# A third tile in the ring for finished blocks, output weights in five single steps, and row maxima as three and one: an attention and feed-forward block on one core

## The chip, the core and the metric

The kernel runs on one core of a Trainium2 chip. Such a core has five engines that run side by side, each with its own queue of instructions, taken in order: TensorE (PE in the profile, its weight loads PEld), VectorE (DVE), ScalarE (ACT), GpSimd (POOL) and SyncE (SP), which here only starts transfers. PE writes its results to PSUM; DVE and ACT read them there and put them into SBUF. Transfers between SBUF and the memory of the chip (DMA) are started from an engine's queue, here those of SP and ACT. Engines wait for each other and for transfers through semaphores. The metric is the time of one execution on the device in microseconds (us); the kernel before takes 2186.95 us as the median of 3 runs (2176.08 to 2189.83).

## The reference

The reference is a transformer block with layer norm ahead of each part, for 2048 tokens of width 640, 32 heads of 20 numbers each, and a feed-forward width of 1728. Cut to its core:

```python
# x: [1, 2048, 640]; wqkv: [640, 1920]; wo: [640, 640]
# w_gate, w_up: [640, 1728]; w_down: [1728, 640]
def attention(x):
    qkv = (x @ wqkv).reshape(B, S, 3, H, Dh).transpose(2, 0, 3, 1, 4)
    q, k, v = qkv[0], qkv[1], qkv[2]
    scores = einsum("bhqd,bhkd->bhqk", q, k) * Dh ** -0.5
    p = softmax(scores, axis=-1)
    o = einsum("bhqk,bhkd->bhqd", p, v)
    return o.transpose(0, 2, 1, 3).reshape(B, S, D) @ wo

h = x + attention(layernorm(x))
out = h + (silu(layernorm(h) @ w_gate) * (layernorm(h) @ w_up)) @ w_down
```

The softmax subtracts the maximum of each row of scores. The kernel finds these maxima in a pass of its own, with scores that are computed for that alone.

## The kernel before

Operands of the matmuls are split in two parts, a rounded one ("hi") and the rest ("lo"), and three products (hi·hi, lo·hi, hi·lo) are added up. The order of the instructions of each engine is that of the program's text: no scheduler moves them. The program has three stages.

**Projections, to about 345 us.** The tokens are taken in four chunks of 512. For each chunk the tokens are normalized, flipped (`flip`, L357, copies the flipped tile through a tile `e`), and multiplied with `wqkv`. Ten *blocks* (`query_key`, L381) compute 128 columns of queries or keys for the 512 tokens with 15 matmuls each (L389); eight *value parts* (`value`, L422) compute values. A finished block stands in one of two PSUM tiles (`ps_one`). `keep` (L403) brings it into a tile `e` of SBUF: ACT copies it out (L232), ACT rounds it (L72), POOL computes the rest (L73). Then it is stored to `qk_d` in the chip's memory. The transfers are started by `store` (L375) on ACT's queue (L378), and always one block late: calling `store` for a block starts the transfers of the one before. `e` comes from a pool with two tiles, so a block's copy waits until the store of the block two earlier has landed. In chunk 0 every third block uses instead `third`, memory borrowed from `v_stk[0]`, which is filled with values only at slot 14 of chunk 3 (`load_values(0)`).

Between these matmuls the stage does part of the row maxima. `visit(n)` (L309) starts the loads that are due (`load_items`, L256; the transfers are those of L118 on SP's queue, from `qk_d` into four `raw` tiles) and takes up to n *pairs* that are ready. A pair (`max_pair`, L141) is two matmuls (L146) into one of three double-width PSUM tiles (`ps_wide`) and one reduction by DVE (L150) over 128x1024 numbers. `visit(2)` stands in the middle of a block (L393, after the ninth matmul) and again after the block; after a value part stands `visit(3)`. In chunks 0 to 2 the work of a chunk is blocks first and then value parts; in chunk 3 it is five blocks of keys, the value parts, and five blocks of queries, so that the stage ends with blocks. DVE also normalizes the next chunk's tokens and splits weights in this stage.

**Attention, about 345 to 1565 us.** There are 32 *units*: 8 groups of four heads by 4 chunks of queries. A unit runs over 16 key tiles. For each, PE computes scores (L642) into one of four PSUM tiles, ACT takes the exponential (L648) into a tile `probs`, and PE multiplies that with the values (`weigh`, L652) two key tiles later. The remaining maxima are interleaved: one matmul (L156) and one reduction by DVE (L162) each. ACT is busy with exponentials nearly all the time, and takes its instructions in order. At the end of a unit row sums are brought into a small tile by four transfers on SP (L665), once a unit.

In unit 27 (`NU - 5`) the five pieces of the output weights `wo` are brought in: `load_wo` (L543) at key tiles 0, 3, 6, 9 and 12 loads a piece into `wo_raw`, which has two buffers, and `split_wo` (L547) at key tiles 2, 5, 8, 11 and 14 splits it, the rounding on ACT and the rest on POOL (L764 to L767). From unit 29 on, output projections for the finished chunks run beside attention.

**Output projection and feed-forward, about 1565 us to the end.** The change doesn't touch this stage.

The lines around which the change is made are these; they set when the pairs are taken, where a block is copied to, and when the output weights come:

```python
if n == 1 and k == 3:
    visit(2)                                  # in query_key, mid-block
...
if c == 0 and m % 3 == 2:                     # in keep
    e = third.bitcast(F32R)
else:
    e = evp.tile([P, 2, CH], F32R, name="e")
...
visit(2 if kind == "block" else 3)            # after a block or a value part
...
if u == NU - 5 and kt % 3 == 0 and kt // 3 < ND:
    load_wo(kt // 3)
```

Of the kernel before, what the change touches and what calls it, by code (L numbers as in the profile page):

```python
# [9 lines left out]
F32 = mybir.dt.float32  # L10
BF16 = mybir.dt.bfloat16
F32R = mybir.dt.float32r
# [5 lines left out]
P = 128  # L18
# [5 lines left out]
ND = D // P  # L24
NT = S // P
CH = 512
# [17 lines left out]
def tile_block(ctx: ExitStack, tc: tile.TileContext, x, wqkv, wo, wg, wu, wd, out):  # L44
# [18 lines left out]
    def ps_one():  # L63
        return psum.tile([P, CH], F32, name="ps_one", tag="ps_one", bufs=2)
# [6 lines left out]
    def split(src, hi, lo, lo_engine=nc.vector):  # L71
        nc.scalar.activation(hi, src, AF.Copy)  # L72
        lo_engine.tensor_tensor(out=lo, in0=src, in1=hi.bitcast(F32), op=ALU.subtract)  # L73
# [24 lines left out]
    NU = NG * NC  # L98
# [3 lines left out]
    v_stk = [stk.tile([P, NT, VG], F32, name="v_stk0")]  # L102
# [113 lines left out]
    evp_ctx = ExitStack()  # L216
    evp = evp_ctx.enter_context(tc.tile_pool(name="evp", bufs=2))
    evs = [evp.tile([P, NG, VG], F32, name=f"ev{i}", bufs=1) for i in range(2)]
    with tc.tile_pool(name="pa", bufs=2) as pa:
        xs = {}  # L220
        zs = {}
# [8 lines left out]
        def split_sbuf(src, hi, lo, copy):  # L230

            nc.scalar.activation(copy, src, AF.Copy)  # L232
            split(copy, hi, lo, nc.gpsimd)
# [75 lines left out]
        def visit(n):  # L309
            load_items()  # L310
            for _ in range(n):
                for queue in (urgent, early):
                    if queue and queue[0][0]():
                        queue.pop(0)[1]()
                        break
# [38 lines left out]
        def flip(c, k):  # L354
            ps = ps_one()
            for t in range(TPC):
                nc.tensor.transpose(  # L357
                    ps[:, t * P : (t + 1) * P], xs[c * TPC + t][:, k * P : (k + 1) * P], ident
                )
            z_hi, z_lo = (z[:, k, :] for z in zs[c])  # L360
            split_sbuf(ps, z_hi, z_lo, evp.tile([P, 2, CH], F32R, name="e")[:, 0].bitcast(F32))

        def flip_tokens(t):

# [10 lines left out]
        def store(*last, queue=nc.scalar):  # L375

            while stores:
                queue.dma_start(*stores.pop(0))  # L378
            stores.extend(last)

        def query_key(c, *ms):  # L381

            z_hi, z_lo = zs[c]
            pss = [ps_one() for _ in ms]
            n = 0
            for a, w in ((z_hi, w_hi), (z_lo, w_hi), (z_hi, w_lo)):
                for ps, m in zip(pss, ms):
                    for k in range(ND):
                        nc.tensor.matmul(  # L389
                            ps, w[:, k, m * P : (m + 1) * P], a[:, k, :],  # L390
                            start=(n == 0 and k == 0), stop=(n == 2 and k == ND - 1),
                        )
                        if n == 1 and k == 3:  # L393
                            visit(2)
                n += 1
            for ps, m in zip(pss, ms):
                keep(c, m, ps)

        third = v_stk[0].rearrange("p t w -> p (t w)")[:, : 2 * CH].rearrange(
            "p (i n) -> p i n", i=2  # L400
        )

        def keep(c, m, ps):  # L403

            if c == 0 and m % 3 == 2:
                e = third.bitcast(F32R)
            else:
                e = evp.tile([P, 2, CH], F32R, name="e")
            split_sbuf(ps, e[:, 0], e[:, 1], e[:, 1].bitcast(F32))
            r0 = m // 2 * P  # L410
            pieces, r = [], r0
            while r < r0 + P:
                g, i = divmod(r, GD)
# [60 lines left out]
        for c in range(NC):  # L474
            lns = []
            work = (some_keys + some_queries if c else first) + parts
            if c == NC - 1:
                work = some_keys + parts + some_queries
            for j, (kind, *which) in enumerate(work):
                slot[0] = 18 * c + j  # L480
                if c == 0 and j < 9:
# [8 lines left out]
                    lns = norm(c + 1)  # L490
                if which:
                    (query_key if kind == "block" else value)(c, *which)
                visit(2 if kind == "block" else 3)
                if c == 0 and j == 6:
                    for ev in evs:
                        nc.gpsimd.memset(ev, 1.0)
# [219 lines left out]
    for u in range(NU):  # L716
        g, c = divmod(u, NC)
# [3 lines left out]
        for kt in range(NT):  # L721
# [33 lines left out]
            if g == NG - 1 and c >= 1:  # L755
# [4 lines left out]
                if NT - 4 <= kt < NT - 1:  # L760
                    ahead[0][kt - NT + 4]()
                    if kt == NT - 4 and c < NC - 1:
                        ahead[4]()
            if u == NU - 5 and kt % 3 == 0 and kt // 3 < ND:  # L764
                load_wo(kt // 3)
            if u == NU - 5 and kt % 3 == 2 and kt // 3 < ND:
                split_wo(kt // 3)  # L767
    for f in extra:
        f()
    while todo:  # L770
# [1 line left out]
    u, o, r = tail.pop()  # L772
# [213 lines left out]
```

## Time and profile before

| what | number |
|---|---|
| time, median of 3 runs (lowest to highest) | 2186.95 us (2176.08 to 2189.83) |
| the profiled execution's own time | 2179.47 us |
| its span in the trace | 2177.5 us |
| TensorE busy | 2133.4 us, 98% of the span, 12882 matmuls |
| VectorE, ScalarE busy | 1612.2 us (74%), 1278.2 us (59%) |
| GpSimd busy | 316.6 us (15%) |
| mean granted clock of TensorE | 0.993 |

A row of the page's fifth part names the line, the engine, the operation and the tiles of a group of instructions, then their count, their busy time and mean duration, and the idle time of the engine just before them with what ended most of it. The trace's timeline shows instructions one after the other: start, duration, engine, line, operation, and in brackets the idle time before and its releaser. "ACTq L378" or "SPq L118" are transfers started from the queue of ACT or SP at that line. The granted clock (PEclk) is a share of TensorE's full speed.

### The profile page before, as it was taken

To read this page: it belongs to the slowest core of one execution; us is meant where nothing else is said; L and a number is where in the kernel's file an instruction comes from. 1 tells how busy PE (TensorE), PEld (TensorE's weight loads), DVE (VectorE), ACT (ScalarE), POOL (GpSimd) and SP (SyncE) were. 2 spreads that over 40 slices of the span, in tenths; PEclk is the share of its full clock that TensorE was granted. 3 is DMA by queue.
4 is the path that set the end of the run, shared out by engine and by line. 5 is a ranking of instruction groups with operands and counts; after the bars stand their busy time and mean duration, and the time that the engine had idled before them with its cause. 6 is when DMAs were issued, how large, how long until landed. Compare 5 with 4: busy or idle time off the path is not lost.

```text
span 2177.5 us, 33846 instructions
## 1 busy us (share of the span) xinstructions
PE 2133.4 (98%) x12882; PEld 1254.7 (58%) x12882; DVE 1612.2 (74%) x2731; ACT 1278.2 (59%) x2486; POOL 316.6 (15%) x282
## 2 busy tenths in 40 slices
PE   7989999999999999999999999999999999999999
PEld 5766764333333333333333333345688888888888
DVE  7988996999999999999999998884353433443434
ACT  4222216999999999999999998876621111121110
POOL 5222212000000000000000001011213222122220
PEclk9999999999999999999999999999999999999999
DMA  8655532110212211102012112111221000010102
GB/s 249 189 155 158 162 105 80 55 50 19 79 26 57 48 36 55 48 21 79 26 54 51 36 55 65 34 58 58 74 64 37 25 25 25 19 31 20 30 19 97
DMA packets 123066, 140.06 MB, mean 64 GB/s; under 512 B 38600, under 2 KB 71624, under 8 KB 122904
## 3 DMA queue, kind: packets, MB, share of 16 engines
q1 hardware_dynamic: 108920, 111.15, 17.8%
q10 hardware_dynamic: 13984, 26.75, 3.9%
q8 instruction: 101, 1.65, 0.3%
q14 instruction: 61, 0.50, 0.1%
HBM read 99.06 MB, written 38.01 MB: 63 GB/s over the span
## 4 chain that ended last, share of the span: by engine, by line
PE 89%; DVE 7%; DMA 3%; ACT 1%; issue 0%; SPq 0%; ACTq 0%; POOL 0%; DVEq 0%; POOLq 0%
PE acc L652 23%; PE ps_a L836 17%; PE ps_max L156 15%; PE ps_one L642 14%; PE ps_b L922 9%; DVE mx L150 4%; PE ps_one L389 3%; PE ps_one L430 2%; PE ps_wide L146 2%; PE ps_max L582 2%; DMA qk_d<-e 1%; PE ps_b L582 1%; DVE mx L162 0%; PE ps_one L357 0%; DMA wo_raw<-in_A_wo 0%
## 5 line engine op out<-in xcount | busy, mean ns | idle before, releaser
L648 ACT ACTIVATE probs<-ps_one 128x512 f32<-128x512 f32 x2048 | 1044.7, 621 | 136.1 <-PE ps_one L642 135.5
L162 DVE TENSOR_REDUCE mx<-ps_max 128x1 f32<-128x512 f32 x1632 | 1020.6, 682 | 109.1 <-PE ps_max L156 74.8
L642 PE MATMUL ps_one<-q_stk,k_stk 62*128 62x512 f32 x2048 | 553.0, 424 | 5.0 <-ACT e L232 4.5
L652 PE MATMUL acc<-probs,v_stk 128*32 128x512 f32 x4096 | 548.1, 607 | 0.2
L156 PE MATMUL ps_max<-k_stk,q_stk 60*128 60x512 f32 x1632 | 543.2, 462 | 1.9 <-DVE mx L162 1.3
L156 PEld LDWEIGHTS ps_max<-k_stk,q_stk 60*128 60x128 f32 x1632 | 231.8, 185 | 431.4 <-DVE mx L162 411.0
L927 DVE TENSOR_TENSOR h<-ps_b,h 128x320 f32<-128x320 f32 x448 | 194.4, 485 | 311.9 <-PE ps_b L922 311.8
L642 PEld LDWEIGHTS ps_one<-q_stk,k_stk 62*128 62x128 f32 x2048 | 301.2, 186 | 83.9 <-ACT probs L648 51.5
L836 PE MATMUL ps_a<-z,gu_hi 128*128 128x512 f32 x1080 | 275.9, 393 | 0.6 <-ACT z L72 0.6
L150 DVE TENSOR_REDUCE mx<-ps_wide 128x2 f32<-128x1024 f32 x208 | 239.6, 1215 | 22.7 <-PE ps_wide L146 22.6
L836 PEld LDWEIGHTS ps_a<-z,gu_hi 128*128 128x128 f32 x1080 | 200.4, 188 | 42.2 <-ACT z L72 0.8
L72 ACT ACTIVATE y_hi<-s 128x512 fp32r<-128x512 f32 (+1 forms) x56 | 35.4, 631 | 253.7 <-DVE s L849 247.2
L652 PEld LDWEIGHTS acc<-probs,v_stk 128*32 128x32 f32 x4096 | 81.0, 108 | 160.8 <-issue 152.4
L844 ACT ACTIVATE s<-ps_a 128x512 f32<-128x512 f32 (+1 forms) x56 | 33.5, 598 | 198.5 <-PE ps_a L836 198.5
L836 PE MATMUL ps_a<-z,gu_lo 128*128 128x512 f32 x540 | 142.2, 393 | 0.0
L922 PE MATMUL ps_b<-d_hi,y_hi 128*128 128x320 f32 x448 | 139.0, 311 | 0.0
L922 PE MATMUL ps_b<-d_lo,y_hi 128*128 128x320 f32 x448 | 138.1, 309 | 0.0
L232 ACT ACTIVATE e<-ps_one 128x512 f32<-128x512 f32 x52 | 31.1, 598 | 168.4 <-DMA qk_d<-e 75.1
L922 PE MATMUL ps_b<-d_hi,y_lo 128*128 128x320 f32 x416 | 128.3, 308 | 0.0
L173 POOL CAST both<-neg 128x16 fp32r<-128x16 f32 x32 | 6.6, 207 | 830.7 <-DVE neg L169 393.6
L836 PEld LDWEIGHTS ps_a<-z,gu_lo 128*128 128x128 f32 x540 | 101.4, 188 | 23.1
L73 POOL TENSOR_TENSOR y_lo<-s,y_hi 128x512 fp32r<-128x512 f32 x52 | 67.9, 1307 | 269.5 <-ACT y_hi L72 269.5
(113 smaller groups left out, 1606.3 us busy)
## 6 DMA issues: line engine op xcount, KB each, us to landing
raw<-qk_d SPq DMA_DIRECT2D x70, 160.0 KB
k_stk<-qk_d SPq DMA_DIRECT2D x64, 160.0 KB
q_stk<-qk_d SPq DMA_DIRECT2D x64, 160.0 KB
qk_d<-e ACTq DMA_DIRECT2D x29, 320.0 KB
rb<-r_d SPq DMA_DIRECT2D x32, 256.0 KB
v_d<-ev ACTq DMA_DIRECT2D x16, 384.0 KB
raw<-qk_d SPq DMA_DIRECT2D x70, 80.0 KB
v_stk<-v_d SPq DMA_DIRECT2D x28, 192.0 KB
```

The source lines that it names most:

```text
L73: lo_engine.tensor_tensor(out=lo, in0=src, in1=hi.bitcast(F32), op=ALU.subtract)
L150: nc.vector.tensor_reduce(mx[:, :, pair, t, kc], ps, axis=AX.X, op=ALU.max)
L156: nc.tensor.matmul(ps, queries[u][rows, pair, t * P : (t + 1) * P], keys[u // NC][rows, pair, kc * CH : (kc + 1) * CH], start=True, stop=True,
L162: nc.vector.tensor_reduce(mxs[u][:, b, pair, t, kc : kc + 1], ps, axis=AX.X, op=ALU.max)
L389: nc.tensor.matmul(ps, w[:, k, m * P : (m + 1) * P], a[:, k, :], start=(n == 0 and k == 0), stop=(n == 2 and k == ND - 1),)
L582: nc.tensor.matmul(ps[:, :HALF], a[:, k, :], w[:, k, hs], start=(n == 0), stop=(n == 3 * ND - 1),)
L642: nc.tensor.matmul(ps, keys[u // NC][rows, p, kt * P : (kt + 1) * P], queries[u][rows, p, :], start=True, stop=True,)
L648: nc.scalar.activation(probs[p][:, b, :], ps, AF.Exp, scale=scale)
L652: nc.tensor.matmul(acc[32 * j : 32 * j + 32, :], values[u // NC][:, kt, j * VW : j * VW + 32], probs[j // 2][:, j % 2, :], start=(kt == 0) ...
L836: nc.tensor.matmul(ps, a[:, i, k, :], b[:, k, :], start=(n == 0), stop=(n == 3 * ND - 1))
L922: nc.tensor.matmul(ps[:, :HALF], a[:, t * P : (t + 1) * P], b[:, hs], start=(n == 0), stop=(n == len(products) - 1),)
L927: nc.vector.tensor_tensor(out=h, in0=ps[:, :HALF], in1=h, op=ALU.add)
```

## The change

The change has three parts.

First, a ring `es` of three tiles takes the place of the pool of two: two tiles of `evp` and the borrowed memory `third`. Every block of every chunk and every flip takes the next tile of the ring (`next_e`). At the start of chunk 3 the borrowed tile leaves the ring, and another tile comes in: a further `z_hi` tile of pool `pa`, of which two of five slices are used.

Second, the pairs of maxima are taken differently around blocks: `visit(1)` in the middle of a block and none there in chunk 0, and `visit(3)` behind every block as behind every value part.

Third, the output weights are loaded at key tiles 12 and 13 of units 24, 25 and 26 (two, two and one piece), and split at key tiles 2 and 3 of the unit after each.

```diff
+    es = [evp.tile([P, 2, CH], F32R, name=f"e{i}", bufs=1) for i in range(2)]
+    es.append(v_stk[0].rearrange("p t w -> p (t w)")[:, : 2 * CH].bitcast(F32R))
+    third = es[2] = es[2].rearrange("p (i n) -> p i n", i=2)
+
+    def next_e():
+        es.append(es.pop(0))
+        return es[-1]
...
-            split_sbuf(ps, z_hi, z_lo, evp.tile([P, 2, CH], F32R, name="e")[:, 0].bitcast(F32))
+            split_sbuf(ps, z_hi, z_lo, next_e()[:, 0].bitcast(F32))
...
-                        if n == 1 and k == 3:
-                            visit(2)
+                        if n == 1 and k == 3 and c:
+                            visit(1)
...
-            if c == 0 and m % 3 == 2:
-                e = third.bitcast(F32R)
-            else:
-                e = evp.tile([P, 2, CH], F32R, name="e")
+            e = next_e()
...
             if c == NC - 1:
                 work = some_keys + parts + some_queries
+
+                es[:] = [e for e in es if e is not third]
+                es.append(pa.tile([P, ND, CH], F32R, name="z_hi")[:, :2])
...
-                visit(2 if kind == "block" else 3)
+                visit(3)
...
-            if u == NU - 5 and kt % 3 == 0 and kt // 3 < ND:
-                load_wo(kt // 3)
-            if u == NU - 5 and kt % 3 == 2 and kt // 3 < ND:
-                split_wo(kt // 3)
+            k = 2 * (u - NU + 8)
+            if kt in (12, 13) and 0 <= k + kt - 12 < ND:
+                load_wo(k + kt - 12)
+            if kt in (2, 3) and 0 <= k + kt - 4 < ND:
+                split_wo(k + kt - 4)
```

More of the change, by code (lines that the diff above doesn't have):

```diff
@@ L397, in query_key @@
                 keep(c, m, ps)
-        third = v_stk[0].rearrange("p t w -> p (t w)")[:, : 2 * CH].rearrange(
-            "p (i n) -> p i n", i=2
-        )
         def keep(c, m, ps):
-            if c == 0 and m % 3 == 2:
-                e = third.bitcast(F32R)
-            else:
-                e = evp.tile([P, 2, CH], F32R, name="e")
+            e = next_e()
             split_sbuf(ps, e[:, 0], e[:, 1], e[:, 1].bitcast(F32))
```

## The prediction

> **What bounds the kernel now.** I begin with the head of the page and the line of the chain of waits by engine.
>
> ```profile
> span 2177.5 us, 33846 instructions
> PE 2133.4 (98%) x12882; PEld 1254.7 (58%) x12882; DVE 1612.2 (74%) x2731; ACT 1278.2 (59%) x2486; POOL 316.6 (15%) x282
> PE 89%; DVE 7%; DMA 3%; ACT 1%; issue 0%; SPq 0%; ACTq 0%; POOL 0%; DVEq 0%; POOLq 0%
> ```
>
> TensorE is busy 2133.4 of 2177.5 us. The change leaves every matmul in place, so all it can win is idle time of TensorE and time spent at a low clock. The view of windows says in which stage that lies (columns: window and its length; busy us and instruction count of PE, PEld, DVE, ACT, POOL; granted clock; DMA share; GB/s).
>
> ```profile
> core 0: us, PE busy (x) PEld busy (x) DVE busy (x) ACT busy (x) POOL busy (x), PEclk, DMA share, GB/s
> 0.00:345.00 345.00, 316.13 (x1583) 225.56 (x1583) 289.58 (x343) 94.69 (x162) 89.74 (x72) 0.98 0.55 168
> 345.00:1565.00 1220.00, 1212.09 (x8108) 496.53 (x8109) 1060.06 (x1786) 1075.09 (x2144) 83.55 (x110) 0.99 0.17 48
> 1565.00:2177.00 612.00, 605.13 (x3193) 532.62 (x3192) 262.55 (x602) 108.39 (x181) 143.35 (x100) 1.00 0.13 38
> ```
>
> The projections (to 345 us) hold 28.9 us of PE idle time, attention 7.9 over 1220 us, and the feed-forward part, which the change doesn't touch, 6.9. Next the view of waits of PE in the projections, and the timeline rows of the longest ones (start, duration, engine, line, tile; in brackets the idle time before it and its releaser).
>
> ```profile
> PE ps_wide L146 <- DVE mx L150: 6.0, 5, 1.9
> PE ps_one L430 <- ACT e L232: 4.6, 2, 3.9
> PE ps_wide L146 <- DMA raw<-qk_d: 3.1, 2, 2.7
> ...
> 127.73 0.51 PE L146 MATMUL ps_wide<-k_stk,q_stk 60*128 60x512 f32 x2 [1.28 <-DVE mx L150]
> 150.20 1.70 PE L430 MATMUL ps_one<-w_hi,z_hi 128*128 128x320 f32 x5 [3.92 <-ACT e L232]
> 197.70 0.58 PE L146 MATMUL ps_wide<-raw 60*128 60x512 f32 x1 [2.73 <-DMA raw<-qk_d]
> 199.34 1.19 PE L146 MATMUL ps_wide<-raw 60*128 60x512 f32 x3 [1.06 <-DMA qk_d<-e]
> 221.88 0.79 PE L146 MATMUL ps_wide<-k_stk,q_stk 60*128 60x512 f32 x2 [1.91 <-DVE mx L150]
> 345.82 0.79 PE L642 MATMUL ps_one<-q_stk,k_stk 62*128 62x512 f32 x1 [4.50 <-ACT e L232]
> 1357.48 0.27 PE L181 MATMUL ps_one<-ident,both 128*32 128x128 f32 x1 [3.52 <-ACT probs L648]
> ```
>
> A stall can cost twice, since the clock drops behind it. These windows lie around those rows:
>
> ```profile
> 150.20:155.00 4.80, 4.80 (x22) 4.19 (x22) 0.35 (x1) 1.49 (x3) 1.27 (x1) 0.65 0.81 241
> 195.00:205.00 10.00, 6.24 (x16) 3.49 (x17) 4.38 (x7) 1.23 (x2) 1.45 (x2) 0.66 0.58 171
> 219.00:226.00 7.00, 5.09 (x16) 3.11 (x14) 6.47 (x14) 1.23 (x2) 1.27 (x1) 0.76 0.52 166
> 345.80:355.00 9.20, 9.18 (x35) 4.75 (x35) 6.33 (x11) 6.89 (x14) 8.29 (x3) 0.50 0.60 169
> 1354.00:1366.00 12.00, 8.52 (x36) 3.15 (x37) 4.32 (x8) 6.43 (x14) 2.78 (x2) 0.72 0.25 74
> ```
>
> Length times the missing clock is the work lost: 4.80 x 0.35 = 1.7 us, 10 x 0.34 = 3.4 (of it about 2.9 outside the idle time), 7 x 0.24 = 1.7, 9.2 x 0.50 = 4.6, 12 x 0.28 = 3.4. The stalls of 1.91 us and longer were followed by a drop. That of 1.28 us was not: the window 89 to 131 below has clock 1.00.
>
> **The change part by part.** All sums are against the profiled execution's own 2179.47 us (span 2177.5 and 2.0 around it), which lies 7.5 us under the median of the runs shown, 2186.95.
>
> *Three tiles in the ring.* A finished block is copied out of PSUM by ACT into a tile, and stored by a DMA. ACT waits for a store before it can reuse the tile.
>
> ```profile
> ACT e L232 <- DMA qk_d<-e: 74.8, 16, 6.2
> 142.91 1.32 ACTq L378 DMA_DIRECT2D qk_d<-e  x2
> 149.55 0.60 ACT L232 ACTIVATE e<-ps_one 128x512 f32<-128x512 f32 x1 [6.02 <-DMA qk_d<-e]
> ```
>
> ACT waits 16 times, 74.8 us in all, but only the waits in the PE rows above reach TensorE: 4.6 us in chunk 1 and 4.5 at 345.82. In chunk 1 the copy at 149.55 waits for the store issued at 142.91, one block late. With three tiles it needs the store issued a block (about 5.5 us) earlier, which has landed near 144; the copy behind it is late by at most half a microsecond, and two PSUM buffers cover that. I take out 4.6 us of idle and 1.7 of clock: **-6.3** (0 to -6.5). Chunk 0 already has the third tile for every third block; its flips go through the ring too but store nothing, so they free their tile by themselves. At chunk 3 the borrowed tile is given back, because v_stk[0] is loaded at slot 14; its last stores are of chunk 2, an entire chunk earlier, so that load waits for nothing.
>
> *The raw tiles in chunk 2.* The stall at 197.70 is on a load from qk_d, 199.34 on a store.
>
> ```profile
> 187.61 0.82 ACTq L378 DMA_DIRECT2D qk_d<-e  x2
> 192.36 2.29 SPq L118 DMA_DIRECT2D raw<-qk_d  x4
> ```
>
> In the built program the load issued at 192.36 waits for the store issued at 187.61, which landed 4.75 us later; after the change it waits only for earlier loads, and so goes out up to about 4 us sooner. That covers the 2.73 and most of the 1.06 us; with the clock, 2.73 + 1.06 + 2.9 = 6.7 at most. I take **-5** (0 to -6.7), as the data of that block may come late all the same.
>
> *Maxima as 3 and 1, and none in mid-block in chunk 0.* This is the costliest part to be wrong on, as DVE sets the pace here. Rows: two windows, the group of reductions, and four matmuls of two pairs.
>
> ```profile
> 46.45:63.00 16.55, 14.05 (x69) 9.37 (x69) 16.55 (x17) 5.78 (x10) 7.97 (x7) 1.00 0.67 210
> 89.00:131.00 42.00, 40.34 (x178) 25.10 (x174) 41.05 (x58) 8.16 (x14) 7.72 (x6) 1.00 0.62 189
> L150 DVE TENSOR_REDUCE mx<-ps_wide 128x2 f32<-128x1024 f32 x208 | 239.6, 1215 | 22.7 <-PE ps_wide L146 22.6
> 130.44 0.73 PE L146 MATMUL ps_wide<-k_stk,q_stk 60*128 60x512 f32 x4
> ```
>
> In chunk 0 DVE is busy all of 46.45 to 63.00 and PE idles 2.5 us of it. The changed order of instructions has 9 pairs in chunk 0's blocks where there were 12, so three reductions leave a DVE-bound stretch. They start about 1.15 us apart (their 1.215 us overlap a little): 3 x 1.15 = 3.4. The three go behind chunk 1's last block, which had none; there DVE has room and PE pays about 0.33 us a pair, 1.0. Together **-2.4** (-3.4 to +1).
>
> In chunks 1 to 3 the count a block stays four, so PE (40.34 of 42.00) and DVE (41.05) stay level. What changes is the shape: three pairs in a row fill all three ps_wide buffers, where two left one free. The first of the three is free again after one pair and one reduction, 0.33 + 1.2 = 1.5 us, and the single pair of the next block comes later than that (it stands behind nine of the block's fifteen matmuls), so it finds a free buffer as long as DVE isn't behind. Where it is behind (1.28 at 127.73, 1.91 at 221.88, with norm's instructions in between), the stall comes sooner and grows by about half a reduction, and one of them may now be long enough to drop the clock for 1.7 us: 2 x 0.4 + 1.7 = **+2.5** (0 to +6).
>
> *The end of the projections.* Here a wait goes and another comes.
>
> ```profile
> 341.00 1.27 ACTq L378 DMA_DIRECT2D qk_d<-e  x2
> 345.17 0.60 ACT L232 ACTIVATE e<-ps_one 128x512 f32<-128x512 f32 x1 [3.60 <-DMA qk_d<-e]
> 347.19 3.54 ACT L648 ACTIVATE probs<-ps_one 128x512 f32<-128x512 f32 x7 [0.76 <-PE ps_one L642]
> ```
>
> Before, the last block's copy waits until 345.17 for the store issued at 341.00, the first scores wait for that copy (its PSUM), and the first exponential starts at 347.19. After, three tiles remove that. But the third tile of chunk 3 is now a z_hi tile, whose memory the first probs tile takes over: in the built program the first exponential waits for the last store out of that tile, and that store is issued on ACT's queue behind the last block's two copies. By the row, PE's last block ends 345.82 - 4.50 = 341.3, the store goes out near 342.0, and lands 345.17 - 341.00 = 4.2 us at most after issue: the exponential starts at about 345.5 to 346.3, not 347.19. Queued behind it on ACT are all other exponentials, and behind those the weighing matmuls; PE has four ps_one buffers and some maxima, about 2 us of work, and then waits. So the stall moves and shrinks by 1 to 1.7 us, and some of the 4.6 us of lost clock may go with it. I take **-3** (+0.5 to -9, the whole of 4.5 + 4.6).
>
> *Output weights over units 24 to 27.* Before, unit 27 loads and splits all five pieces; timeline rows of the loads of row sums, one a unit, give its length.
>
> ```profile
> 1300.11 2.48 SPq L665 DMA_DIRECT2D r<-o  x4
> 1336.19 2.45 SPq L665 DMA_DIRECT2D r<-o  x4
> 1380.29 2.47 SPq L665 DMA_DIRECT2D r<-o  x4
> 1356.12 0.74 ACT L72 ACTIVATE wo_hi<-wo_raw 128x640 fp32r<-128x640 f32 x1 [3.73 <-DMA wo_raw<-in_A_wo]
> ```
>
> Units take 36.1 us, that one 44.1. Its split sits in ACT's queue and waits 3.73 us for its load, the exponentials stand behind it, PE stops (3.52 at 1357.48) and the clock falls. After, a piece is split six or so key tiles after its load in the unit before, about 14 us by 36.1/16 = 2.3 us a key tile, so nothing waits. The five splits remain, 5 x 0.74 = 3.7 us of ACT in a stage where ACT is busy 1075.09 of 1220.00: two in a row, 1.5 us, may put PE back by up to 0.5 us in each of three units. The loads stand on SP between loads needed a unit later. 8.0 less 0.5 to 1.5: **-7** (-6 to -8).
>
> Sum: -6.3 - 5 - 2.4 + 2.5 - 3 - 7 = **-21.2**, own time 2158.3. The runs shown lie from 3.4 under to 10.4 over the profiled execution, their median 7.5 over; a median of the new kernel may stand 0 to 7.5 over its own profile, so 2158 to 2166, and I forecast **2163 us**, 1.1% under the median. About 1% (22 us) is what a measurement of this kernel can tell from no change, so the forecast lies on that edge.
>
> **The rivals.**
>
> *Short stalls cost no clock.* If the clock falls only after stalls above some length, and the changed kernel's are all below it, the terms in which I kept lost clock go too: the 1.7 in chunk 2's rest, the 1.7 in the maxima, and most of the 4.6 at the end, 8 us more: about 2150. For it speaks the 1.28 us stall without a drop; against it that 1.91 us had one. [...]
>
> *DVE and loads take over.* Where the ring's wait is gone, chunk 1 runs into DVE, busy 41.05 of 42.00 us there, and chunk 2's load is late by its data: the ring gives half (-3), the raw tiles nothing, the end nothing: -3 - 2.4 + 2.5 - 7 = -10, own time 2169.5, median 2171 to 2184. This is also how the change would fail to do what it says, with wo alone fully paid.
>
> *Slower: the batch of three stalls PE in every block.* Place: the ps_wide buffers in the 26 or so blocks of chunks 1 to 3 with maxima. If a DVE at 98% never catches up between batches, PE waits in each. The rest of the sum is -23.7; this turns the change slower from 23.7/26 = 0.9 us a block, and by over 1% from (23.7 + 22)/26 = 1.8. At the 1.91 us of the worst stall seen, 26 x 1.91 = 50, +26: 2205. Against it: the same number of reductions a block, and before, PE waited for DVE only five times, 6.0 us.
>
> **How the numbers follow.** Forecast, 2156 to 2171: 0.48. No clock lost, about 2150 (2146 to 2156): 0.15. Takeover, 2171 to 2186: 0.25. Slower, around 2205: 0.07. The rest 0.05. A range of 2147 to 2187 leaves out the slower case, the rest and the edges, under 2 in 10. Faster by over 1% is below 2165: 0.30 of the forecast's 0.48, the 0.15 and 0.03 of the rest, 0.48; slower by over 1%, 0.07; within 1%, 0.45.
>
> **What would show it.** Ring: no PE row with 3.92 before it in chunk 1, and ACT's waits for qk_d stores far under 74.8 us. Raw tiles: no 2.73 near 198 and a clock near 1.0 there. Maxima: waits of PE for DVE mx L150 over 6.0 us, but not in every block. End: the first exponential released by a store out of z_hi, near 345.5 less what came before. Output weights: no wait for wo_raw, and a unit 27 of about 36.5 us. I would be wrong if PE's waits for L150 came in tens, if the exponential started later than before after the last block, or if a new store or load wait took the place of that at 150.20.

## The result and the profile after

The changed kernel takes 2170.29 us (median of 7 runs, 2165.18 to 2174.76) against 2181.7 us for the kernel before (7 runs, 2176.08 to 2189.83, measured together): a ratio of 0.9946 with a 95% interval of 0.9924 to 0.9969, that is 0.3 to 0.8% faster. The profiled execution took 2168.44 us, 11.0 less than that of before, where the prediction's sum had 21.2 less. The page of the kernel after begins so, and the line of the chain of waits by engine follows:

```profile
span 2166.7 us, 33817 instructions
PE 2130.7 (98%) x12882; PEld 1255.5 (58%) x12882; DVE 1612.8 (74%) x2731; ACT 1277.7 (59%) x2486; POOL 316.5 (15%) x282
PE 91%; DVE 5%; DMA 2%; issue 1%; POOL 0%; ACT 0%; SPq 0%; ACTq 0%; POOLq 0%; DVEq 0%
```

The work is the same, and PE is idle for 36.0 us where it was idle for 44.1. The view of waits of PE up to 350 us shows what is left in the projections (us in total, times, longest):

```profile
PE ps_wide L146 <- DVE mx L150: 6.2, 11, 1.8
PE ps_one L646 <- ACT probs L652: 4.5, 1, 4.5
PE ps_wide L146 <- DMA k_stk<-qk_d: 2.2, 2, 1.9
PE ps_one L397 <- ACT e L240: 1.4, 1, 1.4
...
PE ps_wide L146 <- DMA raw<-qk_d: 0.6, 1, 0.6
```

The wait of values for a copy into the ring (4.6 us) has gone, that for raw tiles has shrunk from 3.1 to 0.6 us, waits for DVE have become more and shorter, and the wait at the first scores has become one for the exponential. New are 2.2 us on loads of `k_stk`, 1.87 of them in one wait in chunk 1's blocks. The timeline rows that answer to those of before:

```profile
110.64 0.47 PE L146 MATMUL ps_wide<-raw 60*128 60x512 f32 x1 [0.61 <-DMA raw<-qk_d]
126.69 0.47 PE L146 MATMUL ps_wide<-k_stk,q_stk 60*128 60x512 f32 x1 [1.87 <-DMA k_stk<-qk_d]
185.86 0.82 ACTq L386 DMA_DIRECT2D qk_d<-e  x2
185.98 13.48 SPq L118 DMA_DIRECT2D raw<-qk_d  x12
335.99 2.81 ACTq L386 DMA_DIRECT2D qk_d<-z_hi  x3
342.30 4.03 ACT L652 ACTIVATE probs<-ps_one 128x512 f32<-128x512 f32 x8 [5.74 <-DMA qk_d<-z_hi]
342.95 1.77 PE L646 MATMUL ps_one<-q_stk,k_stk 62*128 62x512 f32 x3 [4.54 <-ACT probs L652]
1296.01 2.47 SPq L669 DMA_DIRECT2D r<-o  x4
1332.84 2.46 SPq L669 DMA_DIRECT2D r<-o  x4
1369.30 2.47 SPq L669 DMA_DIRECT2D r<-o  x4
```

The raw tiles of chunk 2 are now loaded at 185.98, beside the store of 185.86 and not behind it. The first exponential waits 5.74 us for the store out of the z_hi tile. Unit 27 takes 1369.30 - 1332.84 = 36.5 us.

To see where the time went, I cut both traces at the same pieces of work (the first matmul of a block or a value part, the copy of a unit's sums) and took the lengths between the cuts, in us:

| from ... to | before | after | difference | predicted |
|---|---|---|---|---|
| first block of chunk 0 to first block of chunk 1 | 73.4 | 71.5 | -1.9 | -3.4 |
| chunk 1's ten blocks | 53.8 | 59.3 | +5.5 | +1.0, and most of +2.5 |
| chunk 1's first two value parts | 12.5 | 7.3 | -5.2 | -6.3 |
| to the fourth block of chunk 2 | 37.2 | 37.8 | +0.6 | |
| from there to the fifth | 11.8 | 5.5 | -6.3 | -5 |
| the other blocks of chunk 2 | 34.9 | 35.4 | +0.5 | the rest of +2.5 |
| to the end of the last block | 101.6 | 102.3 | +0.7 | |
| from there to the end of unit 0 | 47.4 | 48.4 | +1.0 | -3 |
| units 1 to 24 | 874.3 | 874.7 | +0.4 | 0 |
| units 25 to 28 | 153.9 | 147.6 | -6.3 | -7 |

The differences add up to -11.0, and the rest of the kernel gives 0.2 back: -10.8 of span. Two terms are off by more than 2 us: chunk 1's blocks and the end of the projections.

### The profile page after: what moved, and what is told of

Read it like the earlier page. It is cut to its first block, busy times and chain, and to the rows that moved or that the text cites. A ratio compares the mean times of both kernels' runs of the same rounds, so it can differ in the third digit from the quotient of the medians.

```text
span 2166.7 us, 33817 instructions
## 1 busy us (share of the span) xinstructions
PE 2130.7 (98%) x12882; PEld 1255.5 (58%) x12882; DVE 1612.8 (74%) x2731; ACT 1277.7 (59%) x2486; POOL 316.5 (15%) x282
## 4 chain that ended last, share of the span: by engine, by line
PE 91%; DVE 5%; DMA 2%; issue 1%; POOL 0%; ACT 0%; SPq 0%; ACTq 0%; POOLq 0%; DVEq 0%
PE acc L656 23%; PE ps_a L841 17%; PE ps_max L156 15%; PE ps_one L646 14%; PE ps_b L927 9%; PE ps_one L397 4%; DVE mx L150 3%; PE ps_one L431 2%; PE ps_wide L146 2%; PE ps_max L586 2%; PE ps_b L586 1%; DMA raw<-qk_d 1%; DVE mx L162 0%; PE ps_one L365 0%; PE ps_one L181 0%
## 5 line engine op out<-in xcount | busy, mean ns | idle before, releaser
L72 ACT ACTIVATE y_hi<-s 128x512 fp32r<-128x512 f32 (+1 forms) x56 | 35.4, 631 | 253.7 <-DVE s L854 247.2
L240 ACT ACTIVATE e<-ps_one 128x512 f32<-128x512 f32 x37 | 22.1, 596 | 114.2 <-PE ps_one L397 85.8
```

## The experiments

All times are medians, and ratios are against the kernel before on the same chip. Beside them stand lengths from each kernel's one profile, cut as above: chunk 0, chunk 1's blocks, chunk 1's first two value parts ("ring"), fourth to fifth block of chunk 2 ("raw"), end of the last block to end of unit 0 ("end"), units 25 to 28 ("wo").

| kernel | us | ratio and 95% interval | chunk 0 | chunk 1 | ring | raw | end | wo |
|---|---|---|---|---|---|---|---|---|
| before | 2181.7 | | 73.4 | 53.8 | 12.5 | 11.8 | 47.4 | 153.9 |
| after | 2170.29 | 0.9946 (0.9924 to 0.9969) | 71.5 | 59.3 | 7.3 | 5.5 | 48.4 | 147.6 |
| wo_alone | 2175.7 | 0.9974 (0.9961 to 0.9987) | 79.3 | 53.9 | 8.6 | 10.5 | 47.4 | 147.5 |
| ring_alone | 2173.4 | 0.9958 (0.9941 to 0.9974) | 76.7 | 54.5 | 7.2 | 12.0 | 46.5 | 153.0 |
| maxima_alone | 2180.06 | 0.9983 (0.9972 to 0.9995) | 73.0 | 58.9 | 7.4 | 10.2 | 48.1 | 153.1 |
| ring_and_wo | 2171.63 | 0.9952 (0.9934 to 0.9970) | 73.4 | 52.9 | 7.2 | 12.0 | 46.4 | 147.6 |
| z_hi_earlier | 2165.63 | 0.9931 (0.9917 to 0.9945) | 70.8 | 58.6 | 7.4 | 5.5 | 43.8 | 147.5 |
| two_two_later | 2174.23 | 0.9967 (0.9954 to 0.9979) | 71.7 | 59.3 | 7.4 | 12.1 | 48.2 | 147.5 |
| three_one_from_2 | 2171.46 | 0.9951 (0.9933 to 0.9968) | 75.5 | 59.5 | 7.4 | 5.5 | 48.8 | 147.5 |
| three_one_from_2_z_hi | 2161.15 | 0.9914 (0.9902 to 0.9927) | 70.9 | 58.3 | 7.4 | 5.5 | 42.8 | 147.6 |
| after_turn | 2170.03 | 0.9951 (0.9934 to 0.9968) | 72.1 | 57.0 | 7.4 | 11.0 | 47.5 | 147.6 |
| chunk0_four | 2166.85 | 0.9931 (0.9910 to 0.9952) | 75.4 | 52.9 | 7.2 | 5.5 | 43.7 | 147.6 |
| three_one_from_1 | 2161.56 | 0.9919 (0.9897 to 0.9941) | 73.1 | 57.5 | 7.2 | 6.4 | 43.7 | 147.5 |
| from_1_spare | 2160.21 | 0.9908 (0.9882 to 0.9935) | 74.4 | 55.3 | 7.2 | 8.9 | 43.8 | 147.6 |

How to read it: before and wo_alone have chunk 0 in the same program, and yet it takes 73.4 us in one execution and 79.3 in the other. The blocks of chunk 1 hold 39 pairs in the kernels with three pairs a block in chunk 0, and 36 in the others: three pairs have moved from the one column into the next. A difference of 2 or 3 us between two medians says little; the lengths of the later columns say more, where many kernels agree.

### Each part alone

**wo_alone**, the kernel before with only the output weights spread:

```diff
-            if u == NU - 5 and kt % 3 == 0 and kt // 3 < ND:
-                load_wo(kt // 3)
-            if u == NU - 5 and kt % 3 == 2 and kt // 3 < ND:
-                split_wo(kt // 3)
+            k = 2 * (u - NU + 8)
+            if kt in (12, 13) and 0 <= k + kt - 12 < ND:
+                load_wo(k + kt - 12)
+            if kt in (2, 3) and 0 <= k + kt - 4 < ND:
+                split_wo(k + kt - 4)
```

> The kernel before with only the output weights spread over units 24 to 27. By the ledger of the two traces, units 24 to 27 take 147.57 us after and 153.88 us before, so theory: about 6.3 us faster, unit 27 36.5 to 37.5 us long, no wait for wo_raw. Rival: the gain is given back later in attention, because the splits delay exponentials in three units; then 2 us or less is left.

Measured: 0.9974, 3 to 9 us faster, and units 25 to 28 in 147.5 us, as in every kernel that has this edit; without it they take 153.0 to 153.9. The gain isn't given back: units 1 to 24 take 874.2 to 875.0 us in all fourteen profiles. Where the splits now stand, units 25 and 26 take 0.6 and 0.8 us more in the trace after (37.3 and 36.9 for 36.7 and 36.1).

**ring_alone**, with only the ring (in query_key and behind it the old visits):

```diff
-                e = evp.tile([P, 2, CH], F32R, name="e")
+            e = next_e()
```

> The kernel before with only the ring of three tiles; maxima as two and two, output weights in unit 27. Theory: the ring removes both the stall at 150.2 (5.1 us in the ledger) and that at 197.7 (5.8), and costs 0.9 at the end of the projections: about 10 us faster, last block's first matmul near 327.7 instead of 337.7. Rival: the stall at 197.7 went because the pairs are taken at other places; then it stands here too, and only 4 us are won.

Measured: 9 us faster, as the theory said, but not for its reason. The value parts take 7.2 us, but the fourth block of chunk 2 still takes 12.0: the rival's part. The profile of ring_alone, the timeline of PE:

```profile
198.72 0.76 PE L146 MATMUL ps_wide<-raw 60*128 60x512 f32 x1 [3.29 <-DMA raw<-qk_d]
200.03 1.19 PE L146 MATMUL ps_wide<-raw 60*128 60x512 f32 x3 [0.55 <-DMA raw<-qk_d]
```

So the ring alone doesn't remove this stall.

**maxima_alone**, with only the visits changed:

```diff
-                        if n == 1 and k == 3:
-                            visit(2)
+                        if n == 1 and k == 3 and c:
+                            visit(1)
...
-                visit(2 if kind == "block" else 3)
+                visit(3)
```

> The kernel before with only the maxima as three and one, none in mid-block in chunk 0. Theory: 2 us won in chunk 0, 5 to 6 lost in the blocks of chunks 1 and 2, together 3 to 4 us slower, with the clock lowered behind the stall near 127 and with idle time of PE behind the batches of three near 110. Rival: the loss in chunk 1 comes of the ring, which makes raw loads late there; then this is 1 to 2 us faster.

Measured: 1 to 6 us faster, against the theory. Its loss in chunk 1 is there (58.9 us for 53.8), and the stall in chunk 2 shrinks only to 10.2. What the theory didn't have is the value parts: 7.4 us, without any ring. The stall that the ring was to remove is absent here. The kernel before shows how much it hangs on the execution: in wo_alone, whose program is the same up to attention, these parts take 8.6 us, not 12.5.

**ring_and_wo**, the changed kernel with the old visits:

> The changed kernel with the maxima as two and two as before (in chunk 0 too). Theory: the sum of the ring and the output weights, 10 + 6.3 = 16 us faster than the kernel before, about 5 faster than the whole change. Rival (three and one costs nothing, its chunk 0 part wins): 2 us slower than the whole change, 9 faster than before.

Measured: 2171.63 us, 6 to 14 faster than before, and no different from the changed kernel. Here chunk 1's blocks take 52.9 us and lose nothing, and the fourth block of chunk 2 takes 12.0 with the stall. In the changed kernel it is the other way round, and these two nearly cancel. So the stall in chunk 2 is gone only with the ring and the new visits together, and the new visits cost about as much in chunk 1.

### What decides the stall in chunk 2

In the traces of before and after, the 1105 transfers of this program (991 on SP's queue, 114 on ACT's) name eight semaphores, 138 or 139 transfers each, and the orders of both queues fit one common turn through the eight. Some loads stand behind a store whose data they don't read. In the profile after, the token loads, which read `x`, wait for stores of values; what SP's queue waits for from 80 to 345 us (us in total, times, longest):

```profile
SPq L236 <- DMA v_d<-ev: 9.7, 2, 4.9
```

One of them goes out at 97.76, right after the store of 92.34, the one before it on its semaphore, has landed at 97.69; a load of `k_stk` goes out at 120.12, after the store of 116.12, the one before it on its semaphore, has landed at 120.10. In the kernel before, the first load of raw tiles behind chunk 2's token loads, at 192.36, has the turn of the store of the block before, issued at 187.61 and landed at 192.30, and by the built programs it has that in ring_and_wo, maxima_alone and two_two_later, too; in the changed kernel the one at 185.98 has that of an older load, landed at 182.92. One spare transfer moves the turns of the later ones on by one. **after_turn**, the changed kernel with it:

```diff
+    spare = [const.tile([1, 16], F32, name=f"spare{i}") for i in range(1)]
+
+    def spare_load(n):
+        for _ in range(n):
+            nc.sync.dma_start(spare.pop(), x[0:1, 0:16])
...
                     if c > 0:
+                        spare_load((0, 0, 1)[c])
                         load_x(c + 1)
```

> The changed kernel with one spare transfer (64 bytes from x into a tile that nobody reads) on SP's queue ahead of chunk 2's token loads, so that every later transfer moves on by one among the eight counters that transfers share in turn. In the built program the last token load then waits for the store of the block before, the first load of raw tiles behind it too, and its fourth piece for the store of the block after that. Theory (the stall near 197.7 is decided by which store a load's counter is shared with): the stall is back, 2 to 5 us of idle time of PE between 190 and 202 with half clock behind it, 4 to 8 us slower than the changed kernel, 2174 to 2178. Rival (it is the order of the pairs, three behind a block, that removed the stall): no stall, 2169 to 2172.

The profile of after_turn, the timeline of the queues of SP and ACT, then that of PE (this kernel has six lines more ahead, so L124 is L118, L392 is L386):

```profile
183.27 6.44 SPq L242 DMA_DIRECT2D xt<-in_A_x  x4
185.00 0.82 ACTq L392 DMA_DIRECT2D qk_d<-e  x2
189.85 9.71 SPq L124 DMA_DIRECT2D raw<-qk_d  x12
...
194.56 0.47 PE L152 MATMUL ps_wide<-raw 60*128 60x512 f32 x1 [1.46 <-DVE st L100]
196.66 0.76 PE L152 MATMUL ps_wide<-raw 60*128 60x512 f32 x1 [1.63 <-DMA raw<-qk_d]
```

The token loads last 6.44 us here for 1.77 in after (from 183.95 on), since, by the built program, the last waits for the store of 185.00, and the raw loads come at 189.85. Of PE's two waits, the first ends with an instruction of DVE (statistics of tokens, `st`), the second with the load. The stall is back, and the fourth block takes 11.0 us where it took 5.5, with the visits and the ring untouched. That settles the cause in the trace. The time doesn't show it: 2170.03 us, where I expected 2174 to 2178. This execution is 2.3 us shorter in chunk 1's blocks and 0.9 at the end. The feed-forward part is shorter, too, though the edit wasn't meant to touch it. The costliest group of its matmuls, in after and then in after_turn:

```profile
L841 PE MATMUL ps_a<-z,gu_hi 128*128 128x512 f32 x1040 | 265.7, 393 | 0.6 <-ACT z L72 0.6
L848 PE MATMUL ps_a<-z,gu_hi 128*128 128x512 f32 x1040 | 263.0, 390 | 0.6 <-ACT z L78 0.6
```

From the first of these matmuls (into `ps_a`) to the last it takes 572.7 us here and in from_1_spare, the other kernel with a spare transfer and its tile, and 577.4 to 577.5 in the twelve kernels without: 4.8 us less, which hide most of the stall's 5.5. With them added, this kernel would take 2174.8 us (an estimate), inside the range expected. Why these matmuls are faster beside a spare tile isn't shown.

### What costs 5 us in chunk 1

**two_two_later**: the changed kernel with two and two from chunk 1 on, and three a block in chunk 0.

```diff
-                        if n == 1 and k == 3 and c:
-                            visit(1)
+                        if n == 1 and k == 3 and c:
+                            visit(2)
...
-                visit(3)
+                visit(2 if kind == "block" and c else 3)
```

> The changed kernel with two and two pairs in chunks 1 to 3, and chunk 0 as changed (three behind a block, none in the middle). In the built program the first load of raw tiles behind the token loads of chunk 2 waits again for the store of the block before. Theory: the stall of 2 to 4 us with half clock near 192 is back (5 to 6 us against the changed kernel), and the 5 us that the changed kernel loses in the blocks of chunk 1 is not lost: about the same time as the changed kernel. Rival: three and one is a gain by itself; then this is 3 us or more slower than the changed kernel.

The stall in chunk 2 is back (12.1 us), but the blocks of chunk 1 are as slow as in the changed kernel, 59.3 us, with two and two. So it isn't the batch of three. Its waits of PE from 89 to 143 us:

```profile
PE ps_wide L146 <- DMA raw<-qk_d: 2.4, 2, 1.2
PE ps_wide L146 <- DVE mx L150: 1.4, 1, 1.4
```

**three_one_from_2** (two and two in chunk 1 alone) tells the same: `visit(1 if c > 1 else 2)` in the block and `visit(2 if kind == "block" and c == 1 else 3)` behind it.

> The changed kernel with two and two pairs in chunk 1 alone; chunk 0 as changed, three and one from chunk 2 on. In the built program the load named above waits for earlier loads only, as in the changed kernel. Theory: no stall near 190 and no loss in chunk 1: 4 to 5 us faster than the changed kernel, about 2165.5, 17 us under the kernel before. Rival: the loss in chunk 1 is DVE's in any shape; then the same as the changed kernel.

No stall in chunk 2 (5.5 us), as expected; but 59.5 us in chunk 1. The rival's time came, 2171.46 us, though not its reason: PE waits 2.37 us for raw tiles there, and for DVE 1.39, hardly more than the 1.28 of the kernel before.

What these kernels share is three pairs a block in chunk 0. That moves the turns, too: in the changed kernel the third token load of chunk 1 has the turn of a store of values. The queues of SP and ACT in the profile after:

```profile
91.91 6.66 SPq L236 DMA_DIRECT2D xt<-in_A_x  x4
98.66 6.32 SPq L118 DMA_DIRECT2D raw<-qk_d  x6
...
92.34 0.36 ACTq L386 DMA_DIRECT2D v_d<-ev  x1
```

and in the profile before:

```profile
89.95 2.71 SPq L228 DMA_DIRECT2D xt<-in_A_x  x4
94.46 6.21 SPq L118 DMA_DIRECT2D raw<-qk_d  x8
```

The token loads take 6.66 us for 2.71, and the raw loads behind them start 4.2 us later. In the changed kernel the longest wait in these blocks, 1.87 us at 126.69, comes of a further turn: two of four loads of `k_stk` wait for the pieces of the store of 116.12, and go out at 120.12 and 121.65, 0.02 us after these have landed. The profile after, and then the profile before:

```profile
116.12 1.36 ACTq L386 DMA_DIRECT2D qk_d<-e  x3
116.87 5.47 SPq L118 DMA_DIRECT2D k_stk<-qk_d  x4
```

```profile
117.12 2.19 SPq L118 DMA_DIRECT2D k_stk<-qk_d  x4
```

Not all of the 5.5 us is waiting. PE's idle time in these blocks grows from 2.3 to 4.3 us and the clock loses 1.7 (3.41 us at clock 0.50 from 127.11 on); the other 1.9 are work at full clock, for 39 pairs in place of 36. **chunk0_four** has two and two in chunks 0 and 1, three and one from chunk 2 on, and the other tile order of the next part:

```diff
-                        if n == 1 and k == 3 and c:
-                            visit(1)
+                        if n == 1 and k == 3:
+                            visit(1 if c > 1 else 2)
...
-                visit(3)
+                visit(2 if kind == "block" and c < 2 else 3)
```

> Ring and output weights as changed, two and two pairs in chunks 0 and 1 as before the change, three and one from chunk 2 on, and the z_hi tile second in chunk 3's ring. In the built program the token loads of chunk 1 wait for earlier loads only; in the changed kernel one of them waits for a store of values. Theory: the 4 to 5 us lost in chunk 1's blocks in all kernels with three pairs a block in chunk 0 come of late raw loads and are not lost here, and 2 us of chunk 0 are: 2 to 3 us faster than the same kernel with three pairs a block in chunk 0 (2161), about 2158.5. Rival (DVE has too much to do in chunk 1 in any order): 2 us slower than that, 2163.

Chunk 1's blocks take 52.9 us, and chunk 2's fourth block 5.5: both losses are gone, as the theory said (three of the pairs are back in chunk 0, which takes 75.4 us). The median is 2166.85 us, not 2158.5. Its six runs stand at 2160.5 and 2161.1 and at 2166.6 to 2168.2, and its profile, one of the short ones (2161.12 us), lost 2.83 us in one wait in chunk 0. What sets the two groups apart isn't settled.

**three_one_from_1** takes three and one already in chunk 1 (`c > 0` for `c > 1` above, `c == 0` for `c < 2`), and **from_1_spare** is the same with one spare transfer ahead of chunk 1's token loads.

> As the kernel with two and two in chunks 0 and 1, but three and one from chunk 1 on. Theory: the shape by itself costs 0 to 1.5 us in the blocks of chunk 1 (the batch of three fills the buffers, DVE is level with PE), far from the 5 us of the changed kernel; 2158 to 2161. Rival (the shape is what costs 5 us in chunk 1): 2162 to 2165, with idle time of PE behind DVE near 110.

> Two and two in chunk 0, three and one from chunk 1 on, z_hi second in chunk 3's ring, as in the last but one kernel, with one spare transfer of 64 bytes on SP's queue ahead of chunk 1's token loads. In the built program the second piece of the first raw tile of chunk 1 then waits for an earlier load, not for a store of values. Theory: the idle time of 2.04 us at 110.71 on a raw tile and the half clock behind it go, chunk 1's blocks lose 1.5 us at most against the kernel before instead of 4.6, and what is left is the price of the shape. Rival (three in a row is what costs it): idle time of 1.5 us or more stays near 110, released by DVE, and 4 us are lost again.

In three_one_from_1 the second piece of chunk 1's first raw tile has the turn of the store of values, and PE's row is that of a late load:

```profile
110.71 0.47 PE L146 MATMUL ps_wide<-raw 60*128 60x512 f32 x1 [2.04 <-DMA raw<-qk_d]
```

In from_1_spare, the only rows of PE with idle time before them from 104 to 131 us are these:

```profile
106.71 0.50 PE L152 MATMUL ps_wide<-raw 60*128 60x512 f32 x2 [0.29 <-DVE mx L156]
130.46 0.50 PE L152 MATMUL ps_wide<-k_stk,q_stk 60*128 60x512 f32 x2 [1.75 <-DVE mx L156]
```

three_one_from_1 takes 57.5 us in chunk 1's blocks, from_1_spare 55.3, with the same order of pairs. The wait of 2.04 us on the raw tile is gone with the turn, and the lengths differ by 2.2 us; but after and after_turn, in the same program up to there, differ by 2.3, so this size is that of one profile each. What is left over the 53.6 us that the five kernels with two and two in chunks 0 and 1 take on the mean (53.8, 53.9, 54.5, 52.9, 52.9) is 1.7 us, as much as the 3.41 us at clock 0.50 cost in after; a drop behind the stall at 130.46 would be worth that (an estimate). So three in a row costs about 0 to 1.7 us in chunk 1, as far as these profiles tell. Beside that, from_1_spare has a smaller stall in chunk 2 (8.9 us there), whose cause stays open.

### The end of the projections

**z_hi_earlier** puts the z_hi tile second in chunk 3's ring, so that its last block is the eighth of ten, not the ninth:

```diff
-                es.append(pa.tile([P, ND, CH], F32R, name="z_hi")[:, :2])
+                es.insert(1, pa.tile([P, ND, CH], F32R, name="z_hi")[:, :2])
```

> The changed kernel, but the z_hi tile comes second in chunk 3's ring, so the last block that uses it is the eighth of ten, not the ninth. Theory: the first exponential waits only for the store of the block before, which is issued near 332.5 in the trace after and lands near 337; it starts at about 337 to 338.8 instead of 342.30, PE's stall of 4.54 us shrinks to 0 to 1.5, and of the 10.24 us at half clock a part goes: 4 to 9 us faster than the changed kernel, about 2163 against 2170. Rival: something else than that store is late at the end of the projections (another tile's memory, the copies of the maxima), and the exponential starts no sooner than 340.

ACT's rows in its profile:

```profile
330.90 1.27 ACTq L386 DMA_DIRECT2D qk_d<-z_hi  x2
333.64 0.60 ACT L240 ACTIVATE e<-ps_one 128x512 f32<-128x512 f32 x1 [2.17 <-PE ps_one L397]
334.33 1.29 ACTq L386 DMA_DIRECT2D qk_d<-e  x3
335.74 4.51 ACT L652 ACTIVATE probs<-ps_one 128x512 f32<-128x512 f32 x9 [0.84 <-DMA qk_d<-e]
```

The exponential starts 0.84 us behind ACT's last copy instead of 5.74, and the end takes 43.8 us for 48.4: 4.6 us, all in this place. The median is 2165.63 us, 4.7 under the changed kernel, though the intervals of the two ratios overlap. Part of the 4.6 us belongs to the changed kernel's execution. Its store out of the z_hi tile takes 2.81 us to issue (335.99 in the profile after); ring_alone, ring_and_wo and after_turn have the same store, in the same three pieces, and issue it in 1.2 to 1.3 us. The profile of ring_and_wo:

```profile
336.48 1.29 ACTq L386 DMA_DIRECT2D qk_d<-z_hi  x3
341.47 2.06 ACT L652 ACTIVATE probs<-ps_one 128x512 f32<-128x512 f32 x4 [4.42 <-DMA qk_d<-z_hi]
```

In these three the end takes 46.4 to 47.5 us, so against them the new order is worth 2.6 to 3.7. **three_one_from_2_z_hi** joins it with three_one_from_2:

> Both of these: two and two in chunk 1 alone, and the z_hi tile second in chunk 3's ring. Theory: the sum of the two gains, 8 to 14 us faster than the changed kernel, 2157 to 2162. Rival: the two end up waiting for the same thing at the end of the projections, and it is no faster than the better one alone.

2161.15 us, a ratio of 0.9914 (0.9902 to 0.9927). It beats the kernel before, and by its ratio the changed kernel, too. three_one_from_1 and from_1_spare stand close to it, but the interval of the first reaches well into that of the changed kernel, and the second has the shorter feed-forward part of the spare tile, 4.8 us. The second gain that was expected in it, chunk 1's, didn't come (58.3 us). Against three_one_from_2 it is 10 us faster by the medians and 14.2 by the spans of the two profiles, of which the end explains 6.0 (48.8 to 42.8); 4.6 lie in chunk 0, 75.5 against 70.9 us in the same program.

## Why the prediction was right or wrong

The forecast, 2163 us, lies 7.3 us under the time measured, and its sum, -21.2 us, is twice the -11.0 of the profiles; the range 2147 to 2187 holds the result because it is wide, not because the terms were right. (The allowance for a median over its profile, 0 to 7.5 us, came to 1.9.) By its steps:

- **Output weights, -7:** -6.3 in the trace, and confirmed alone. Mechanism and size were right.
- **Ring in chunk 1, -6.3:** -5.2 in the trace. The wait fell as described, but its size before was that of one execution (another has 1.3 us where this one had 5.1), and maxima_alone shows none without the ring. The step that failed is taking a single stall of a single profile as the part's worth.
- **Raw tiles in chunk 2, -5:** -6.3, with the mechanism described: the load no longer waits for a late store. But the prediction didn't say of which edit that comes, and it comes of none alone: it is a matter of the turns on this program's eight semaphores, which ring and visits move together; a spare transfer alone made the fourth block's 5.5 us 11.0 again.
- **Maxima, -2.4 and +2.5:** the step that failed. Chunk 0 gave what was said: the seven profiles with three pairs a block take 72.2 us on the mean, those with four 75.1, so -2.9. But chunk 1's blocks lost 5.5 us where 1.0 and most of 2.5 were set down. The three pairs that moved there, 1.0 by the prediction, are 1.9 of it. The rest I looked for in the shape of the batch (DVE, the buffers), which is worth about 0 to 1.7 us. It lay mostly in SP's queue: token loads behind a store of values and `k_stk` loads behind a store of a block, by the very mechanism that I had read in chunk 2 and not looked for in chunk 1. PE's waits for loads there grew from 0.3 to 2.8 us, and the half clock behind the longest costs 1.7. Chunks 2 and 3 lost 0.6 + 0.5 + 0.7 = 1.8 us, which is what +2.5 was meant for.
- **End of the projections, -3:** +1.0. The wait that takes the place of the old one was named rightly, with its engine and tile, and mis-sized. The store did go out 0.7 us after PE's last block, at 335.99. But I took its landing, 4.2 us, from a store in two pieces, and this one has three: in ring_alone, ring_and_wo and after_turn the exponential starts 4.7 to 5.0 us after the store's beginning, and the end takes from 1.0 us less to 0.1 more than before, not 3 less. In the changed kernel it starts 6.3 us after it. There the issue of the third piece takes 1.99 us instead of 0.47, as it takes 1.71 and 2.60 in two_two_later and three_one_from_2; what holds it up isn't shown. The upper end of the term's range, +0.5, was nearly right.

The rival in which DVE and loads take over gave 2169.5 us for the profiled execution, and it took 2168.44; but its terms (ring halved, raw tiles nothing, end nothing) weren't those that came about, so the sum was met by chance. The slower rival, a stall in each of 26 blocks, isn't seen: PE waits for DVE 11 times, 6.2 us. The rival of a clock that ignores short stalls falls, too: the stall of 1.87 us at 126.69 was followed by half clock for 3.41 us (127.11 to 130.53, clock 0.50). (Its 2150 was also an own time, 2158.3 - 8, set beside medians.)

## What to carry to other kernels

Here one spare transfer of 64 bytes made raw loads that it has nothing to do with wait for a late store, and a block's 5.5 us became 11.0 (after_turn). Look in the built program for what each load waits for, in every stage, before pricing an edit by what it does at its own place. When a tile's memory is taken over by the next stage, let the blocks that write it be early ones: the order of three tiles in a ring was worth 2.6 to 4.6 us here, by the profile it is set beside. A stall that one profile shows may be much smaller in the next execution of the same program (5.1 us in before, 1.3 in wo_alone), so a term that rests on one stall deserves a range down to nothing. Where a kernel is changed only to test a cause, compare the stages that it shouldn't touch, too: here the two kernels with a spare tile were 4.8 us shorter in the last one.

## What the runs showed of the hardware

**Half clock came in stretches of 3.41, 6.83 or 10.24 us.** In before these begin at 150.12 (3.41 us), 197.91 (6.83), 221.80 (3.41), 344.68 (10.24) and 1358.44 (6.83), in after at 127.11 (3.41), 215.86 (3.41) and 338.74 (10.24); a last one in each is cut off by the end of the trace. Within each execution they begin at multiples of 3.41 us from each other: 14, 21, 57 and 354 of them from the first in before, 26 and 62 in after. I divided both executions into such windows, from 20 to 1600 us. In the windows just ahead of the drops PE was busy for 0.00, 0.68, 1.57, 0.05 and 0.96 us in before, and for 1.54, 1.67 and 2.19 in after. No other full-clock window of the two had PE busy for less than half, and nine others with 59 to 74% were followed by full clock. What decides between these and the 2.19 us (64%) isn't shown.

Two stalls of nearly the same length cost 1.7 us of clock in one kernel and nothing in another. The first fence is after, whose stall of 1.75 us ends at 214.94 and lies in one window of 3.41 us; the second is z_hi_earlier, whose stall of 1.73 us ends at 214.74 and is cut in two at 214.14, by the windows that I counted for that execution:

```profile
212.44:215.86 3.42, 1.67 (x9) 0.93 (x9) 3.21 (x9) 1.23 (x2) 1.26 (x1) 1.00 0.67 175
215.86:219.27 3.41, 3.41 (x11) 2.18 (x9) 2.94 (x4) 0.00 (x0) 0.00 (x0) 0.50 0.64 213
```

```profile
210.73:214.14 3.41, 2.28 (x12) 1.30 (x10) 2.96 (x16) 1.23 (x2) 0.42 (x1) 1.00 0.38 119
214.14:217.55 3.41, 2.81 (x13) 1.90 (x13) 3.41 (x4) 0.00 (x0) 0.84 (x1) 1.00 0.78 178
217.55:220.97 3.42, 3.42 (x17) 2.16 (x18) 3.15 (x4) 1.23 (x2) 0.07 (x1) 1.00 0.60 214
```

PE is busy 1.67 of 3.42 us in the first window of after, and the next has clock 0.50; in z_hi_earlier it is busy 2.28 and 2.81, and all stay at 1.00. That the edge makes the difference is my reading of this one pair.

**Chunk 0 isn't the same twice.** Up to the first block of chunk 1 the program of the kernel before took 73.4 us in one execution and 79.3 in wo_alone. Their timelines of PE differ most in one wait, ahead of the same matmul, the first here of before and the second of wo_alone:

```profile
47.72 0.50 PE L146 MATMUL ps_wide<-k_stk,q_stk 60*128 60x512 f32 x2 [1.22 <-DVE mx L150]
```

```profile
54.35 0.79 PE L146 MATMUL ps_wide<-k_stk,q_stk 60*128 60x512 f32 x2 [5.94 <-DVE mx L150]
```

In the second the clock averages 0.62 from 51.00 to 60.00, which makes about 6.8 us at half clock (9.00 x 0.38 / 0.5); in before it is 1.00 from 50.00 to 59.00. Such differences, 5.9 us here, are as large as most of the terms of this change, and blur every median above.
